# Output layer of two of ten token tiles as seven block products for eight, its sums on VectorE

## The chip, the cores and the metric

The kernel runs on one core of one Trainium2 chip. The metric is the device time of one execution in microseconds (us), as the median of several runs. A profile is one execution recorded by the hardware profiler; its times are counted from the first instruction (the span). Engines are named as in the profile: PE (TensorE matmuls), PEld (its weight loads), DVE (VectorE), ACT (ScalarE), POOL (GpSimd) and SP, which here only issues DMAs.

## The reference, cut to what matters

Sliding-window causal attention (window 64) over 8 batches, 8 heads, 576 tokens and head size 64, followed by a gated feed-forward layer:

```
scores = q @ k.T / 8, kept where 0 <= row - col < 64; attn = softmax(scores)
x = attn @ v                      # as 4608 tokens x 512
g = relu(x @ w_gate) * (x @ w_val)   # 4608 x 1536
out = g @ w_out                   # 4608 x 512, float32
```

The kernel works in fp16 operands with fp32 accumulation.

## The kernel before, in words

**Tiles.** The 4608 tokens are cut into ten tiles: tiles 0 to 3 of 384 tokens and tiles 4 to 9 of 512 tokens (in the code `NS` = 4 and `LAST` = 9). This text numbers tiles from 0, so the eighth and ninth tile are tiles 7 and 8. Of a wide tile the PE does, in this order: the hidden layer (three groups, `j` = 0, 1, 2, in `fast_hidden`), then the output layer (`fast_output`), with the attention work of later tiles put between the parts of the output layer. Ahead of parts 0 and 1 of the output of tile t come the two halves of `values` of tile t + 1 (matmuls L422, three PSUM banks each), and ahead of parts 2 and 3 two calls of `scores` of tile t + 2 (matmuls L253, four banks each). Tile 7 still has both (values of 8, scores of 9); tile 8 has the values of 9 only; tile 9 has neither.

**A group of the hidden layer.** Each group forms four blocks of 128 hidden features for all 512 tokens. The value half x @ w_val is done as seven block products for eight (P1 to P7, 256 columns each, L573): the features and the tokens are split in halves, and sums of blocks are kept ready in `vs` (of the weights, by `w_form` on POOL, L480) and `xc` (of the tokens, by `x_form` on DVE, L459). Products that are shared are copied out of PSUM on ACT (`snap`, L593) and added on DVE (`add`, L600, PSUM plus SBUF, result `vsum`, four buffers). The gate half is four ordinary 512-column products (L582), with a relu on ACT (L586). The product gate times value is then written to `g_sb`, in four pieces that this text calls (n, h): n = 1 or 0 for the upper or lower half of the features, h = 1 or 0 for the second or first half of the tokens. Piece (1, 0) is written by DVE directly from PSUM (`direct`, L613); (1, 1), (0, 0) and (0, 1) are written by POOL (L606), in this order, each from a sum that DVE has made. The sum for (0, 0) is the group's first, the sum for (1, 1) its second, the one for (0, 1) its last. PE's last product of a group, P3, adds into a bank that the DVE sum of (1, 1) must have read first.

**The output layer.** Four parts of 128 tokens, each twelve matmuls of 512 columns over the feature blocks in the order of `F_LAST` (the group j = 2 last, and of it (0, h) last: matmuls 11 and 12 of a part). Each part is copied out of PSUM by ACT (L663) and stored by a DMA on SP's queue.

**Attention on DVE.** Per half of `values`: three reciprocals (L436), three normalisations out of three banks (L441; each frees its bank), one transpose (L447), then the `xc` sums (L459). Per `scores`: four exponentials on ACT (L389, each frees a bank) and four mask products on DVE (L394).

**What sets the order.** Every engine takes its instructions in a fixed order. A `Weaver` writes it: the PE program advances a planned clock, and the other engines' work is queued with `W.at(time, fn)` at planned times and comes out in that order; `bank()` and the `done` tables make it come out earlier where the program needs it. So a plan's times decide only who stands behind whom; on the chip an engine then waits for whatever its next instruction needs. POOL is in this order too: it issues the loads of q and k (L173) and of v (L199), copies v rows between partitions (L208, L210), forms `vs`, and writes the g pieces. A load into a q or k buffer waits until DVE has transposed what the buffer held before.

**Buffers.** `g_sb` has two buffers, `o_sb` three, `snap` five, `vsum` four; the eight PSUM banks go round in a list `free`.

Of the kernel before, what the change touches and what calls it, by code (L numbers as in the profile page):

```python
# [46 lines left out]
def kernel(  # L47
# [23 lines left out]
    WT = 512  # L71
    NS = 4
    NL = (NT - NS * TT) // WT
    assert NT == NS * TT + NL * WT and TT % 128 == 0
# [20 lines left out]
    vs = persist.tile([128, 4, 2, 128 * HF], FP16)  # L95
    qTs = [persist.tile([128, 2, S, 2], FP16, name=f"qT{i}") for i in range(2)]
# [307 lines left out]
    def t_pv(t, hh, banks, give):  # L404

        if t not in wides:
            wides[t] = {"pv": {}, "give": give, "x": a_n.tile([128, 2, WS, 2, D // 2], FP16, name="xw", bufs=1),
                        "r": a_n.tile([128, 2, WS, 1], FP32, name="rw")}
        d = wides[t]
        d["pv"][hh] = banks  # L410
        unread.update(map(id, banks))
        for qh in range(2):
            qd = 2 * (t - NS) + qh
            while quads[qd].get("masked", 0) < G:
                W.pop()
            for i in range(QW):
                b, vw = divmod(q_window(qd, i), NG)
                for s in range(2):
                    n = 2 * (QW * qh + i) + s
                    to = banks[n // BS][:, VW * (n % BS):]  # L420
                    for j in range(G):
                        nc.tensor.matmul(to[32 * j:32 * j + 32, 0:D + 1],  # L422
                                         quads[qd]["p"][j][:, QW * hh + i, 32 * s:32 * s + 32],
                                         v16s[b % 2][:, vw, G * hh + j, 0:D + 1],
                                         start=True, stop=True, skip_group_check=True)
# [48 lines left out]
    def w_form(n, j):  # L474

        c = slice(256 * j, 256 * j + 256)
        f = slice(256 * j + 128 * HF, 256 * j + 128 * HF + 256)
        a11, a12, a21, a22 = wv[:, 0:2, c], wv[:, 2:4, c], wv[:, 0:2, f], wv[:, 2:4, f]
        x, y, op = ((a21, a22, ADD), (vs[:, 0, :, c], a11, SUB), (a11, a21, SUB), (a12, vs[:, 1, :, c], SUB))[n]
        nc.gpsimd.tensor_tensor(vs[:, n, :, c], x, y, op)  # L480

# [65 lines left out]
    def fast_hidden(t):  # L547
# [7 lines left out]
        def group(j):  # L555
# [40 lines left out]
            def add(delay, to, name, last, n, h):  # L596

                def summed():
# [5 lines left out]

                    def mult():
                        nc.gpsimd.tensor_tensor(gh[:, 2 * j + HF * n:2 * j + HF * n + 2, h], rh[:, 2 * n:2 * n + 2, h], pair(v), MUL)  # L606
                        done[2 * j + HF * n, h] = done[2 * j + HF * n + 1, h] = True
                    W.at(max(W.clock, at["relus", n]) + 0.7, mult)
# [30 lines left out]
            add(0.1, "C", "u2", True, 0, 1)  # L639

        for j in range(NF // 4):
            group(j)

    F_LAST = [f for j in range(NF // 4) for f in (2 * j + HF, 2 * j + HF + 1, 2 * j, 2 * j + 1)]

    def fast_output(t, between):

        g_sb, done = gs[t]
        for sub, before in enumerate(between):
# [11 lines left out]
            def evac(op=op, sub=sub):  # L661
# [3 lines left out]
                nc.sync.dma_start(out[bass.ds(starts[t] + sub * 128, 128)], o_sb)  # L665
            W.at(W.clock, evac)

# [28 lines left out]
    def output_last(t):  # L696
# [3 lines left out]
        for c0, c1, queue in ((0, 256, nc.sync), (256, 384, nc.sync), (384, DM, nc.scalar)):  # L700
# [4 lines left out]
            o_sb = consts.tile([128, c1 - c0], FP32, name=f"o_last{c0}")  # L705
            nc.scalar.copy(o_sb, op[:, 0:c1 - c0])
            queue.dma_start(out[bass.ds(starts[t] + last * 128, 128), c0:c1], o_sb)
# [11 lines left out]
    with tc.manual_schedule():  # L719
# [12 lines left out]
        zero = consts.tile([128, 512], FP16)  # L732
        nc.vector.memset(zero, 0.0)
        zero32 = consts.tile([128, 384], FP32)
# [89 lines left out]
        for u in (4, 5):  # L824
            W.at(52.0, lambda u=u: v_spread(u, pool))
        pair(2, 55.5, 58.5, 61.9)
# [22 lines left out]
        LAST = NS + NL - 1  # L849
        SLOTS = (2.6, 6.53 + 0.8, 6.53 + 2.6, 2 * 6.53 + 0.8)  # L850

        def ahead(t):
# [9 lines left out]
            if t == NS - 1:  # L862
                qk_ahead(NS + 1, T + 11.5, (0.0, 1.4, 8.0, 9.4))
                for qd, x in ((0, 6.0), (1, 9.2), (2, 22.6), (3, 25.8)):
# [34 lines left out]
        for t in range(NS, NS + NL):  # L899
# [10 lines left out]
            if t == LAST:  # L910
                fast_output(t, between[:-1])
                W.drain()
                output_last(t)
            else:
# [32 lines left out]
```

## Time and profile before

| what | value |
|---|---|
| median of 3 runs | 321.8 us (321.8 to 322.2) |
| the profiled execution | 322.06 us, its span 320.2 us |
| mean granted TensorE clock | 0.995 |
| PE busy | 308.8 us, 96% |
| DVE busy | 203.2 us, 63% |
| POOL busy | 177.8 us, 56% |
| ACT busy | 158.1 us, 49% |
| output layer of tile 7, first part to the last | 243.31 to 255.95 us, with attention between |
| output layer of tile 8 | 276.18 to 287.38 us, with one half of values between |

The times of one execution are read from its span; what lies around it is 1.86 us. The chain that ended last is PE's for 89% of the span. A matmul's own duration in the profile (379 ns at 512 columns) overlaps with the next one's: twelve take 2.70 us together, and what one costs is the distance between two starts.

### The profile page before, as it was taken

The numbers are of one execution on the slowest core, as the hardware profiler recorded it, in microseconds if no ns is written. First come the engines' busy times: TensorE is split into PE (matmuls) and PEld (weight loads), VectorE is DVE, ScalarE is ACT, GpSimd is POOL, SyncE is SP. The second block draws the span as 40 slices with busy tenths as digits, with TensorE's granted clock in tenths as the row PEclk, the third lists the DMA queues.
The fourth block names the chain that finished last, engine by engine and source line by source line (L and its number), as shares of the span: only waits on it lengthen the run. The fifth ranks groups of instructions, "written<-read, shape, count | busy, mean of one in ns | idle before, by whom it ended". The sixth has DMA issues, their size and how long they took to land.

```text
span 320.2 us, 9481 instructions
## 1 busy us (share of the span) xinstructions
PE 308.8 (96%) x4077; PEld 190.1 (59%) x4077; DVE 203.2 (63%) x397; ACT 158.1 (49%) x310; POOL 177.8 (56%) x206
## 2 busy tenths in 40 slices
PE   4799999999899999999999999999999999999996
PEld 2586958655546555665566556655665566546654
DVE  6937962667993996779576857686337734643420
ACT  3644325533524616752765276627652666326632
POOL 8859336215988506799168925980495036404540
PEclk9889999999999999999999999999999999999999
DMA  8999998946299149806910691039001100020002
GB/s 218 183 196 205 194 120 161 171 98 99 30 174 165 21 90 160 57 1 104 219 36 0 97 220 43 2 50 127 35 0 34 69 34 3 2 98 35 0 33 102
DMA packets 52491, 29.52 MB, mean 92 GB/s; under 512 B 38880, under 2 KB 43872, under 8 KB 52448
## 3 DMA queue, kind: packets, MB, share of 16 engines
q0 software_dynamic: 46688, 18.29, 49.3%
q1 hardware_dynamic: 5616, 10.55, 9.3%
q8 instruction: 32, 0.52, 0.7%
q14 instruction: 11, 0.09, 0.1%
q10 hardware_dynamic: 144, 0.07, 0.1%
HBM read 37.75 MB, written 9.44 MB: 147 GB/s over the span
## 4 chain that ended last, share of the span: by engine, by line
PE 89%; DVE 3%; ACT 2%; POOL 2%; DMA 2%; issue 1%; DVEq 0%; POOLq 0%
PE bank L658 19%; PE bank L582 19%; PE bank L538 17%; PE bank L573 17%; PE bank L673 10%; PE bank L253 3%; PE bank L422 2%; DVE p L292 2%; DMA v<-in_v_dram 2%; ACT pw L389 1%; PE bank L311 1%; DVE g_sb L525 1%; PE bank L703 1%; POOL v L199 1%; DVE qT L193 0%
## 5 line engine op out<-in xcount | busy, mean ns | idle before, releaser
L606 POOL TENSOR_TENSOR g_sb<-r,vsum 128x512 f16<-128x512 f32 x54 | 68.1, 1276 | 77.7 <-DVE vsum L600 75.7
L600 DVE TENSOR_TENSOR vsum<-bank,snap 128x512 f32<-128x512 f32 x54 | 37.3, 691 | 60.1 <-PE bank L573 36.5
L582 PE MATMUL bank<-xt,wg 128*128 128x512 f16 x288 | 73.9, 379 | 0.0
L658 PE MATMUL bank<-wo,g_sb 128*128 128x512 f16 x276 | 62.9, 380 | 0.0
L586 ACT ACTIVATE r<-bank 128x512 f32<-128x512 f32 x72 | 43.2, 600 | 32.3 <-PE bank L582 32.3
L658 PEld LDWEIGHTS <-g_sb 128*128 128x128 f16 x276 | 25.5, 98 | 28.9
L582 PEld LDWEIGHTS <-wg 128*128 128x128 f16 x288 | 28.2, 98 | 18.6
L525 DVE TENSOR_TENSOR g_sb<-r,bank 128x384 f16<-128x384 f32 x48 | 25.9, 550 | 20.3 <-PE bank L538 18.8
L522 ACT ACTIVATE r<-bank 128x384 f32<-128x384 f32 x48 | 23.7, 496 | 29.4 <-PE bank L538 20.3
L573 PEld LDWEIGHTS <-vs 128*128 128x128 f16 x288 | 28.0, 98 | 15.6 <-issue 1.6
L538 PE MATMUL bank<-xt,wg 128*128 128x192 f16 (+1 forms) x256 | 36.5, 296 | 0.5 <-DVE g_sb L525 0.4
L663 ACT COPY o_sb<-bank 128x512 f32<-128x512 f32 x23 | 13.5, 586 | 45.2 <-PE bank L658 43.2
L593 ACT COPY snap<-bank 128x512 f32<-128x512 f32 x54 | 31.6, 586 | 8.4 <-PE bank L573 8.4
L199 POOL DMA_DIRECT2D v<-in_v_dram x41 | 34.7, 865 | 1.8 <-DMA q<-in_q_dram 1.0
L538 PE MATMUL bank<-xt,wv 128*128 128x192 f16 (+1 forms) x256 | 34.3, 286 | 0.0
L673 PE MATMUL bank<-wo,g_sb 128*128 128x512 f16 x144 | 32.8, 379 | 0.2 <-DVE g_sb L525 0.2
L538 PEld LDWEIGHTS <-wg 128*128 128x128 f16 x256 | 24.3, 102 | 9.8 <-issue 0.9
L573 PE MATMUL bank<-xc,vs 128*128 128x256 f16 x216 | 29.4, 272 | 0.4 <-ACT snap L593 0.4
L208 POOL COPY v<-v 64x512 f16<-64x512 f16 (+1 forms) x22 | 16.1, 732 | 23.7 <-DMA v<-in_v_dram 22.6
L538 PEld LDWEIGHTS <-wv 128*128 128x128 f16 x256 | 22.9, 98 | 8.1
L394 DVE TENSOR_TENSOR pw<-pw,mask 128x512 f16<-128x512 f16 x48 | 20.2, 437 | 11.2 <-ACT pw L389 10.5
L389 ACT ACTIVATE pw<-bank 128x512 f16<-128x512 f32 x48 | 25.9, 608 | 1.5 <-PE bank L253 1.0
(69 smaller groups left out, 358.6 us busy)
## 6 DMA issues: line engine op xcount, KB each, us to landing
out_dram<-o_sb SPq DMA_DIRECT2D x35, 256.0 KB, 3.0
k<-in_k_dram POOLq DMA_DIRECT2D x15, 288.0 KB, 5.3
q<-in_q_dram POOLq DMA_DIRECT2D x15, 288.0 KB, 7.3
v<-in_v_dram POOLq DMA_DIRECT2D x31, 128.0 KB, 8.0
wg<-in_moe_w_gate_dram POOLq DMA_DIRECT2D x6, 256.0 KB, 6.4
wv<-in_moe_w_val_dram POOLq DMA_DIRECT2D x6, 256.0 KB, 8.2
wo<-in_moe_w_out_dram POOLq DMA_DIRECT2D x3, 512.0 KB, 11.9
v<-in_v_dram POOLq DMA_DIRECT2D x10, 64.0 KB, 5.9
```

The lines of the kernel that those rows point to most:

```text
L199: nc.gpsimd.dma_start(v16s[b % 2][lo:hi, g, :, 0:64], v[b, :, 64 * g - 64 + lo:64 * g - 64 + hi].rearrange("h p d -> p h d"))
L389: nc.scalar.activation(d["p"][g].rearrange("p n c -> p (n c)"), d["st"][g], ACT.Exp, scale=scale)
L525: nc.vector.tensor_tensor(g_sb[:, f:f + w, c0:c0 + n], part(r_sb), part(h2), MUL)
L538: nc.tensor.matmul(h[:, b * n:b * n + n], wt[:, c, (f + b) * 128:(f + b) * 128 + 128], xt[:, c, c0:c0 + n], start=(c == 0), stop=(c == NC ...
L573: nc.tensor.matmul(at[to][:, HT * i:HT * i + HT], w[:, k, 128 * i:128 * i + 128], x[:, k], start=(first and i == 0 and k == 0), stop=(k == ...
L582: nc.tensor.matmul(to, wg[:, k, 128 * ff:128 * ff + 128], xt[:, k], start=(k == 0), stop=(k == NC - 1))
L586: nc.scalar.activation(r4[:, n], to, ACT.Relu)
L593: nc.scalar.copy(at[name], at["A"])
L600: nc.vector.tensor_tensor(v, at[to], at[name], ADD)
L606: nc.gpsimd.tensor_tensor(gh[:, 2 * j + HF * n:2 * j + HF * n + 2, h], rh[:, 2 * n:2 * n + 2, h], pair(v), MUL)
L658: nc.tensor.matmul(op, g_sb[:, f, 128 * sub:128 * sub + 128], wo[:, f], start=(i == 0), stop=(i == NF - 1))
L673: nc.tensor.matmul(op, g_sb[:, f, bass.ds(sub * 128, 128)], wo[:, f], start=(f == 0), stop=(f == NF - 1))
```

## The change

In tiles 7 and 8 the output layer becomes seven block products for eight. The 512 tokens and the 512 output columns are each split in two halves, and the 1536 features into upper and lower. Each of the seven products covers 256 tokens, 768 features and 256 columns: twelve matmuls of 256 columns, so 84 matmuls of 256 columns in place of 48 of 512.

- Block sums of the output weights, `ws`, four for each of three groups, are made once by POOL (`wo_form`, 128x512 fp16): six are planned from 50.5 us, six at the planned start of tile 3 plus 15.0 to 23.4 us.
- Block sums of g, `s_sb`, four for each of three groups and each of the two tiles, are made by DVE (`g_form`, 128x512 fp16). The four of a group are planned into the next group, those of group 2 into the output layer.
- In group 2 of these tiles the piece (0, 0) of g is written by DVE in place of POOL.
- Three products are copied out by ACT (`snap`), three results are summed and one copied into `o_sb`: the three sums on DVE, the copy on ACT. The stores are of 256 columns by 256 tokens.
- The products P1, P2, P5 and so on accumulate in three banks (A, B, C) that are held over several products, where before one bank was held at a time. In tile 7 `scores` comes after the first half of P2 and after P4, and the second half of `values` after P5.
- In all wide tiles the first half of a tile now holds its even tokens, the second its odd ones: the weights of the L422 matmuls are read with a step of two elements, and stores go to every second row.
- The zeros for the warm-up matmuls lie in `ws`, and the last part of tile 9 takes its three output buffers from `o_sb` in place of buffers of its own.

The order of instructions on DVE, ACT and POOL is else what it was. On POOL, the first six weight sums stand before and after the four v copies that begin at 45.44 us in the profile of before; the other six stand behind the q load that is issued at 122.92 us, five of them ahead of the v loads of tile 5's keys and values, and the sixth between these loads and the first three g products of tile 4. On DVE, in tiles 7 and 8, the order from the second sum of group 2 on is: sum of (1, 1), `direct`, g sum, sum of (0, 1), product (0, 0), g sum, three reciprocals, g sum, three normalisations, transpose, g sum, three reciprocals, `xc`, three normalisations, transpose; then in tile 7 three masks and three `xc` sums before the first two output sums, in tile 8 one `xc` sum before the first. In tile 7 the first `scores` takes two banks that the second half of `values` gives back (by its first and second normalisation).

```diff
-                                         quads[qd]["p"][j][:, QW * hh + i, 32 * s:32 * s + 32],
+                                         quads[qd]["p"][j][:, QW * hh + i, s:64:2],
...
+    def wo_form(n, j):
+        ...
+        nc.gpsimd.tensor_tensor(to[:, n], x, y, SUB)
...
+    def blocks_out(t):
+        return LAST - 2 <= t < LAST
+
+    def g_form(t, n, j, eng):
+        ...
+        for f, h in (((f1, 0), (f2, 0)), ((f1, 1),), ((f1, 0), (f1, 1)), ((f2, 1),))[n]:
+            while (f.start, h) not in done:
+                W.pop()
+        ...
+        x, y, op = ((a21, a22, ADD), (to[:, 0], a11, SUB), (a11, a21, SUB), (a12, to[:, 1], SUB))[n]
+        eng.tensor_tensor(to[:, n], x, y, op)
...
+                    late = blocks_out(t) and j == NF // 4 - 1 and (n, h) == (0, 0)
...
-                        nc.gpsimd.tensor_tensor(gh[:, 2 * j + HF * n:2 * j + HF * n + 2, h], rh[:, 2 * n:2 * n + 2, h], pair(v), MUL)
+                        (nc.vector if late else nc.gpsimd).tensor_tensor(gh[:, 2 * j + HF * n:2 * j + HF * n + 2, h], rh[:, 2 * n:2 * n + 2, h], pair(v), MUL)
...
+            if blocks_out(t):
+                late = j == NF // 4 - 1
+                for n, x in ((2, 6.6), (0, 7.2), (1, 7.3), (3, 10.4)) if late else ((2, 9.9), (0, 10.0), (1, 10.1), (3, 10.9)):
+                    W.at(T + x, lambda n=n: g_form(t, n, j, nc.vector))
...
+    def block_output(t, after):
...
+        run(0)
+        product("P1", "A", True)
+        snap("a1")
+        product("P5", "C", True)
+        run(1)
+        product("P6", "A", False)
+        snap("u2")
+        product("P2", "B", True, (0,))
+        run(2)
+        product("P7", "A", False)
+        snap("u3")
+        add(0.9, "C", "u3", False, 0, c2)
+        product("P2", "B", False, (1,))
+        add(0.1, "B", "a1", True, 1, c1)
+        product("P4", "A", False)
+        W.at(W.clock, direct)
+        run(3)
+        while ("summed", "u3") not in at:
+            W.pop()
+        product("P3", "C", False)
+        add(0.1, "C", "u2", True, 1, c2)
...
-            o_sb = consts.tile([128, c1 - c0], FP32, name=f"o_last{c0}")
+            o_sb = f_sb.tile([128, DM], FP32, name="o_sb")[:, 0:c1 - c0]
...
+        for j in range(NF // 4):
+            for n in range(2):
+                W.at(50.5 + 1.2 * (2 * j + n), lambda n=n, j=j: wo_form(n, j))
...
+                for j in range(NF // 4):
+                    for n in range(2, 4):
+                        W.at(T + 15.0 + 1.2 * (2 * j + n), lambda n=n, j=j: wo_form(n, j))
...
+            elif blocks_out(t):
+                block_output(t, between)
```

In `block_output`, `run(0)` and `run(1)` are the two halves of `values`, `run(2)` and `run(3)` the two calls of `scores`; P1, P2 and P4 read g, P5, P6, P7 and P3 read the g sums 0, 1, 2 and 3 of all three groups.

## The prediction

> **What bounds the kernel now.** I read the chain that ended last first, then the busy times of each tile, then the time lines of POOL and DVE where the change inserts work.
>
> ```profile
> PE 89%; DVE 3%; ACT 2%; POOL 2%; DMA 2%; issue 1%; DVEq 0%; POOLq 0%
> ```
>
> ```profile
> core 0: us, PE busy (x) PEld busy (x) DVE busy (x) ACT busy (x) POOL busy (x), PEclk, DMA share, GB/s
> 124.90:157.15 32.25, 31.82 (x488) 18.81 (x487) 25.69 (x49) 19.69 (x37) 25.17 (x28) 1.00 0.75 90
> 223.08:255.95 32.87, 32.87 (x439) 19.56 (x437) 18.15 (x38) 18.49 (x33) 15.76 (x15) 1.00 0.09 34
> 255.95:287.38 31.43, 31.43 (x311) 18.62 (x309) 15.01 (x30) 14.36 (x25) 11.30 (x9) 1.00 0.09 35
> ```
>
> These stretches are tiles 4, 7 and 8. PE has no idle time in 7 and 8: matmuls taken away there shorten the run, and every wait given to PE lengthens it. Over a whole tile POOL and DVE have room, but the mean hides the places. In tile 4 POOL is 25.17 of 32.25 us busy, and this is what lies ahead of its output layer:
>
> ```profile
> 122.92 0.53 POOL L173 DMA_DIRECT2D q<-in_q_dram  x1 [1.69 <-DVE xc L459]
> 123.44 4.22 POOL L199 DMA_DIRECT2D v<-in_v_dram  x5
> 129.67 1.31 POOL L606 TENSOR_TENSOR g_sb<-r,vsum 128x512 f16<-128x512 f32 x1 [2.02 <-DVE vsum L600]
> 131.34 2.65 POOL L606 TENSOR_TENSOR g_sb<-r,vsum 128x512 f16<-128x512 f32 x2 [0.35 <-ACT r L586]
> ...
> 136.29 1.28 POOL L606 TENSOR_TENSOR g_sb<-r,vsum 128x512 f16<-128x512 f32 x1 [0.55 <-DVE vsum L600]
> ...
> 143.31 2.51 POOL L606 TENSOR_TENSOR g_sb<-r,vsum 128x512 f16<-128x512 f32 x2
> ```
>
> ```profile
> 144.45 2.70 PE bank L658 x12
> ```
>
> The last POOL row writes (1, 1) and (0, 0) of group 2 and ends at 145.82. PE's matmul 11 of the first output part reads (0, 0), and stands at 144.45 + 10 x 0.225 = 146.7. So POOL has 0.9 us to spare there, and 2.02 + 0.35 + 0.55 = 2.9 us of waits before: 3.8 in all.
>
> **The matmuls.** Twelve 512-column matmuls without attention between take 7.88 / 3 us (36 in 7.88 at 279.50), so 48 take 10.5; by the gate rows (four in 0.86) 10.3. Eight 256-column ones take 0.87 (L573), so 84 take 9.2. The gain is 1.2 us a tile, 2.4 in two, if nothing waits. The 36 further weight loads are covered: the 0.87 rows already have a load for each matmul.
>
> **Six weight sums ahead of tile 4.** The nearest row is w_form's, of the same shape and engine:
>
> ```profile
> L480 POOL TENSOR_TENSOR vs<-wv x6: 1152/1212/1269, 77.1 to 99.8; 128x512 f16<-128x512 f16 x6
> ```
>
> Their starts lie 1.22 us apart (77.11, 78.33), so six take 7.3 us. They stand behind the q load of 122.92, which waits for DVE and cannot come earlier, and ahead of the v loads or the first product. Less the 3.8 to spare, (0, 0) is late by 3.5 us, and PE waits that long, partly in the groups (a fifth `vsum` waits for the first product), the rest at matmul 11. This is the lower end. For the upper end see how a DVE operation with two SBUF operands runs beside POOL:
>
> ```profile
> 147.96 1.30 POOL L606 TENSOR_TENSOR g_sb<-r,vsum 128x512 f16<-128x512 f32 x1
> ```
>
> ```profile
> 148.28 1.29 DVE L459 TENSOR_TENSOR xc<-xt 128x512 f16<-128x512 f16 x1
> ```
>
> It took 1.29 us, where the median of this line is 0.42, and ended 0.31 after POOL's. The sums out of PSUM (L600, 670 to 693 ns in all 54) show nothing of it. In after, eight masks (123.58 to 130.7) meet a POOL that is never idle; if five of them come between the sums and hold POOL for 0.3 us each, it is 1.5 more: 5.0. I take 4.5, as the row shows the exclusion but not who goes first. Tile 5 gets nothing further: its products begin 9.16 us after POOL's last load of v.
>
> [...]
>
> **The first six weight sums** cost nothing. POOL idles 9.7 us before 45.44 and takes two there; four push the q and k loads from 48.4 to 53.3, which land 5 to 7 us later, and DVE first reads them at 66.65. The v copies of 62.05 move to 67 to 69 and are read by PE at 86.1. Without that cover it would be up to 4.9.
>
> **DVE in tile 7.** Lines from group 2 on:
>
> ```profile
> 240.82 0.69 DVE L600 TENSOR_TENSOR vsum<-bank,snap 128x512 f32<-128x512 f32 x1 [1.63 <-ACT snap L593]
> 241.43 0.69 DVE L613 TENSOR_TENSOR g_sb<-r,bank 128x512 f16<-128x512 f32 x1
> 243.41 0.33 DVE L436 RECIPROCAL rw<-bank 128x2 f32<-128x2 f32 x3
> 243.66 1.30 DVE L441 TENSOR_TENSOR xw<-bank,rw 128x128 f16<-128x128 f32 x3
> 245.00 1.25 DVE L447 STREAM_TRANSPOSE xt<-xw 128x1024 f16<-128x1024 f16 x1
> ```
>
> From start to start: a sum 0.61, three reciprocals 0.25, three normalisations 1.34, a transpose 1.28; an fp16 sum 0.34 (250.97 to 251.30 among the xc sums); the moved product I take as a PSUM sum, 0.61 (below it only if SBUF operands are quicker, above it 1.29 by the blocked row). All times are in the clock of before. *Group 1's sums* stand between 239.1 and the sum of (1, 1) at 240.82, but the fourth needs POOL's last product of group 1, which ends at 241.03. So the sum of (1, 1) starts at 241.4; with the exclusion, in which the first sum waits for one product and the next for another, at 242.3. PE's P3 needs it and goes to 242.2 or 243.0 from 242.09. *The chain* from there to the second normalisation of the second half of values: 0.61 + 0.61 + 0.34 + 0.61 + 0.61 + 0.34 + 0.25 + 0.34 + 1.34 + 1.28 + 0.34 + 0.25 + 0.34 + 0.95 = 8.2, plus 0.85 in which the first g sum waits for POOL's product (1, 1) (1.27 us long, started only when the sum is done). It ends at 250.4; with the exclusion one more sum waits for a product (1.25), 252.6. *PE* wants the scores, which need that bank, after P3 (0.44), values, P1, P5, values, P6, half of P2 (0.62 + 0.62 + 42 x 0.109 = 5.8): at 248.5, or 250.5 with its own wait in P5. It waits 2.0 or 2.1 us. After the scores it wants P3 4.5 us later (0.62 + 30 x 0.109 + 0.62), at 255.0 or 257.1; DVE has still 0.61 + 1.28 + six fp16 operations at 0.34 + 0.61 + 0.69 = 5.2 us to go before P3's bank is read, 255.7 or 257.8. P3 takes 1.3, and tile 8 starts at 257.1 or 259.2 against 255.95: the gain has gone, and tile 7 is **1.1 to 3.2 us longer**. I take 2.8, near the upper end, since there POOL's products and DVE's sums meet in nearly every step.
>
> **DVE in tile 8.** POOL has no copies here, group 1's sums fit, and the sum of (1, 1) keeps its 273.69. From it to the end of the output sum that P3 waits for: the first thirteen terms above and the 0.85 (8.1), then three normalisations, transpose, one xc sum and a sum of 0.69, 3.65: 285.4, or 286.7 with one exclusion. PE wants P3 at 276.11 + 72 x 0.109 + 0.62 + 0.1 = 284.7, waits, and ends at 286.8 or 288.0 against 287.38: -0.6 to +0.6; I take +0.4.
>
> **Small edits.** Weights with a step of two elements: kT's (L253) are read so already, and 64 of those matmuls take 0.61 us as 64 of L422 do, so nothing; the far bound, a load stretch of 0.58 us doubled in twelve stretches, is 6.5. Last part of tile 9: the third copy starts at 317.44, and now needs the store issued at 315.4 to have landed; there these take 2.0 us (3.0 over the run), so 0.1, at most 1.0. ACT copies as often as before. The fourth store's buffer waits for the first store, but behind it on DVE stand only masks and a sum of the next tile with a microsecond to spare.
>
> **Sum.** 4.5 + 2.8 + 0.4 + 0.1 = 7.8 us on 322.06, so 329.9 for a profiled execution like that of before; 0.26 less to the median: **329.6**.
>
> **The clock.** In 12:14 PE was busy 1.35 of 2.00 us, with no idle above 0.65, and the granted clock of 14:18 was 0.57. Tile 7's output stage has 3 to 4 us of waits in 16; a loss as at 14:18 is 1.7 us and belongs to the upper end. [...]
>
> **Rivals.**
> - *DVE and POOL hardly exclude each other*: all lower ends, 3.5 + 1.1 - 0.6 = 4.0, so 325.8. For it: the masks of 105 to 107, at 0.41 us beside POOL's copies. Chance 0.25.
> - *Only POOL's queue costs*: g sums and output sums hide as planned, 3.5 - 2.4 = +1.1, so 322.9. It needs DVE operations of about two thirds of my durations. Chance 0.10.
> - *Faster*: the bound stays PE throughout, 321.8 - 2.4 = 319.4. It decides in tile 4: if a weight sum took under 3.8 / 6 = 0.63 us there, as the 64x512 copy does (0.61), POOL would be in time, and DVE would have to be in time too. Chance 0.05.
> - *Dearer weights or clock*: over 332.5. Chance 0.05.
> - The forecast: 0.55.
>
> 0.2% (0.64 us) is about what a measurement can tell from no change. All cases but one are above it, one of them barely: slower 0.93, same 0.02, faster 0.05. The range from 325.2 to 332.5 leaves out the two low rivals and the dear one.
>
> **What would show it.** In after: six POOL sums between 123.4 and 136 and the first product of tile 4 at 135 or later; PE idle some 4 us in tile 4, ended by POOL's g; in tile 7 PE idle about 2 us ahead of the first scores and under 1 ahead of P3, both ended by DVE; fp16 DVE sums of 0.8 to 1.3 us in group 2 and 0.42 elsewhere. A tile 4 without a wait, or output stages of 7 and 8 that are 1 us shorter, would make it wrong.

## The result, and the profile after

The changed kernel takes 333.0 us (median of six runs, 330.9 to 335.8), and the kernel before, on the same chip, 322.4 us: a ratio of 1.033, with a 95% interval of 1.028 to 1.038. The forecast was 329.6 us with a range of 325.2 to 332.5. The direction and the places were right; the size was 3.4 us too small.

The profiled execution took 333.4 us, its span 331.7. Line numbers have moved: the sums from PSUM (L600) are now L635, POOL's g products (L606) L643, the output matmuls (L658) L702, normalisations L443, `xc` sums L461, masks L396, values L424, scores L255. New are L491 (`wo_form`), L514 (`g_form`), L737 (the block products) and L753 (the output sums). First the chain that ended last, from the page of the changed kernel:

```profile
PE 60%; DVE 16%; POOL 15%; issue 6%; DMA 2%; ACT 2%; DVEq 0%; POOLq 0%; ACTq 0%
```

PE had 89% of it before. Now 31% of the span lies on DVE and POOL in this chain. The stretches of tiles 4, 7 and 8, from the table by windows (length, then busy time of each engine, granted clock):

```profile
122.50:163.70 41.20, 37.14 (x502) 20.90 (x501) 31.71 (x52) 22.20 (x41) 34.35 (x36) 0.92 0.75 90
229.61:265.83 36.22, 32.75 (x474) 23.23 (x473) 26.69 (x52) 18.26 (x33) 15.31 (x14) 1.00 0.05 18
265.83:298.58 32.75, 30.88 (x347) 21.99 (x345) 23.62 (x49) 15.08 (x27) 10.39 (x8) 1.00 0.11 36
```

From the first hidden-layer matmul of one tile to that of the next (of tile 9 to the end of the span), the tiles of all kernels in this text have these lengths in us. They carry most of what follows.

| kernel | tile 4 | tile 5 | tile 6 | tile 7 | tile 8 | tile 9 |
|---|---|---|---|---|---|---|
| before | 34.72 | 33.02 | 32.91 | 32.87 | 31.42 | 32.99 |
| after | 41.16 | 33.00 | 32.92 | 36.22 | 32.75 | 33.12 |
| sums early | 34.72 | 32.92 | 32.92 | 36.23 | 32.76 | 33.07 |
| sums only | 38.50 | 33.19 | 32.93 | 32.87 | 31.43 | 34.10 |
| even and odd only | 34.73 | 33.31 | 32.93 | 32.87 | 31.43 | 33.84 |
| wait filled | 38.64 | 33.15 | 32.93 | 36.49 | 32.76 | 33.09 |
| ninth tile only | 34.73 | 33.15 | 32.93 | 32.87 | 32.90 | 33.05 |
| eighth tile only | 34.72 | 32.91 | 32.93 | 36.23 | 31.42 | 33.16 |
| eighth, copies early | 34.72 | 33.12 | 32.93 | 33.97 | 31.41 | 33.12 |
| ninth mended | 34.72 | 32.93 | 32.92 | 32.87 | 30.60 | 33.13 |
| both mended | 34.72 | 33.19 | 32.92 | 33.16 | 30.59 | 33.06 |
| order of B | 34.72 | 33.31 | 32.93 | 31.85 | 30.59 | 33.11 |

So the 11.5 us that the span grew are 6.4 in tile 4, 3.35 in tile 7, 1.3 in tile 8, 0.1 in the last part, and 0.3 before tile 4, whose start lies between 122.27 and 123.53 us in these profiles.

**Tile 4.** POOL's time line, which answers to the one from 122.92 us on of before:

```profile
123.19 0.53 POOL L175 DMA_DIRECT2D q<-in_q_dram  x1 [1.69 <-DVE xc L461]
123.79 1.15 POOL L491 TENSOR_TENSOR ws<-wo 128x512 f16<-128x512 f16 x1
124.90 1.33 POOL L491 TENSOR_TENSOR ws<-wo,ws 128x512 f16<-128x512 f16 x1
...
135.43 3.76 POOL L643 TENSOR_TENSOR g_sb<-r,vsum 128x512 f16<-128x512 f32 x3
...
148.04 2.48 POOL L643 TENSOR_TENSOR g_sb<-r,vsum 128x512 f16<-128x512 f32 x2
```

The first product stands at 135.43 where it stood at 129.67, and POOL runs from then on without a gap until the two products that end at 150.52. PE meets this at matmul 11 of the first output part, as was foreseen, and then something else happens:

```profile
145.26 2.33 PE L702 MATMUL bank<-wo,g_sb 128*128 128x512 f16 x10
150.58 1.03 PE L702 MATMUL bank<-wo,g_sb 128*128 128x512 f16 x2 [2.99 <-POOL g_sb L643]
151.54 1.07 PE L424 MATMUL bank<-v,pw 128*32 128x65 f16 x64
152.55 4.69 PE L702 MATMUL bank<-wo,g_sb 128*128 128x512 f16 x12
```

Twelve matmuls take 4.69 us in place of 2.76, and 64 of the values take 1.07 in place of 0.69. The table by windows of two microseconds, the granted clock in the column after PE's busy time, says why:

```profile
core 0: us, PE busy (x), PEclk, DMA share, GB/s
147.00:149.00 2.00, 0.59 (x3) 1.00 0.00 0
149.00:151.00 2.00, 0.42 (x2) 0.66 0.00 0
151.00:153.00 2.00, 2.00 (x68) 0.50 0.60 61
...
155.00:157.00 2.00, 2.00 (x7) 0.63 1.07 174
157.00:159.00 2.00, 2.00 (x72) 1.00 1.07 256
```

The clock fell to half during the wait and came back some 6.8 us later (1.36 us at 0.50 give the 0.66 of 149:151, and 1.48 of the last at 0.50 the 0.63 of 155:157, with four between). From 150.58 to the first scores at 157.17 are 6.6 us; the same work took 3.9 in a kernel with the same wait and no fall (below). So tile 4's 6.4 us are 0.5 in the groups, 3.15 at the wait and 2.7 of slow clock, to 0.1. By this a wait takes about 0.16 us more than the number in brackets. That is what a matmul's own 0.38 us exceeds the 0.22 from one start to the next, and the matmul ahead of a wait has no next one to overlap with.

**Tile 7.** DVE's time line in group 1 and group 2, two rows of POOL's, and one line of the table of waits of PE from 100 us on (1.6 us in three waits, the longest 1.1):

```profile
239.27 2.06 DVE L514 TENSOR_TENSOR s_sb<-g_sb 128x512 f16<-128x512 f16 x2
...
242.75 0.68 DVE L635 TENSOR_TENSOR vsum<-bank,snap 128x512 f32<-128x512 f32 x1
...
246.98 1.82 DVE L514 TENSOR_TENSOR s_sb<-g_sb 128x512 f16<-128x512 f16 x2
...
252.72 0.68 DVE L643 TENSOR_TENSOR g_sb<-r,vsum 128x512 f16<-128x512 f32 x1
253.44 1.37 DVE L514 TENSOR_TENSOR s_sb<-g_sb 128x512 f16<-128x512 f16 x1
```

```profile
238.36 2.68 POOL L643 TENSOR_TENSOR g_sb<-r,vsum 128x512 f16<-128x512 f32 x2
...
252.95 1.58 POOL L643 TENSOR_TENSOR g_sb<-r,vsum 128x512 f16<-128x512 f32 x1 [1.20 <-DVE vsum L635]
```

```profile
PE bank L608 <- DVE vsum L635: 1.6, 3, 1.1
```

Four g sums of group 0 stand ahead of the sum of (1, 1) of group 1 (242.75), and last from 239.27 to 242.8. The first two run beside the two POOL products that begin at 238.36 and take 2.06 us; the other two run beside v copies and take 0.71 and 0.65. PE's P3 of group 1 waits 1.1 us for that sum. The same happens in group 2 with the sums of group 1, and in the output layer PE waits three times more:

```profile
254.87 0.61 PE L737 MATMUL bank<-ws,s_sb 128*128 128x256 f16 x4 [0.92 <-DVE s_sb L514]
...
259.00 0.18 PE L255 MATMUL bank<-qT,kT 32*128 32x64 f16 x1 [0.69 <-DVE xw L443]
259.53 0.66 PE L255 MATMUL bank<-qT,kT 32*128 32x64 f16 x61 [0.35 <-DVE xw L443]
```

**Tile 8.** DVE's last steps, and PE's P3, which waits for an output sum to leave its bank:

```profile
295.60 0.68 DVE L753 TENSOR_TENSOR o_sb<-bank,snap 128x512 f32<-128x512 f32 x1
296.20 0.41 DVE L461 TENSOR_TENSOR xc<-xt 128x512 f16<-128x512 f16 x1
296.54 0.68 DVE L753 TENSOR_TENSOR o_sb<-bank,snap 128x512 f32<-128x512 f32 x1
```

```profile
297.27 1.47 PE L737 MATMUL bank<-wo,s_sb 128*128 128x256 f16 x12 [1.53 <-DVE o_sb L753]
```

PE goes on when the *second* output sum is done, not the first. The first is B's; P3 needs C's.

### The profile page after: what moved, and what is told of

Its sections match the earlier page's. It is cut to its first block, busy times and chain, and to the rows that moved or that the text cites. A ratio compares the mean times of both kernels' runs of the same rounds, so it can differ in the third digit from the quotient of the medians.

```text
span 331.7 us, 9683 instructions
## 1 busy us (share of the span) xinstructions
PE 310.9 (94%) x4149; PEld 196.9 (59%) x4149; DVE 227.5 (69%) x429; ACT 158.2 (48%) x310; POOL 190.5 (57%) x216
## 4 chain that ended last, share of the span: by engine, by line
PE 60%; DVE 16%; POOL 15%; issue 6%; DMA 2%; ACT 2%; DVEq 0%; POOLq 0%; ACTq 0%
PE bank L573 16%; PE bank L617 12%; PE bank L608 11%; PE bank L702 10%; PE bank L797 6%; POOL g_sb L643 6%; POOL v L201 3%; DVE s_sb L514 3%; DVE p L294 2%; DVE xw L443 2%; DVE xt L449 2%; POOL ws L491 2%; PE bank L255 2%; POOL v L212 2%; DMA v<-in_v_dram 2%
## 5 line engine op out<-in xcount | busy, mean ns | idle before, releaser
L643 POOL TENSOR_TENSOR g_sb<-r,vsum 128x512 f16<-128x512 f32 x52 | 66.2, 1290 | 82.9 <-DVE vsum L635 81.3
L635 DVE TENSOR_TENSOR vsum<-bank,snap 128x512 f32<-128x512 f32 x54 | 37.2, 688 | 42.3 <-PE bank L608 27.7
L702 PE MATMUL bank<-wo,g_sb 128*128 128x512 f16 x180 | 43.6, 395 | 3.0 <-POOL g_sb L643 3.0
L617 PEld LDWEIGHTS <-wg 128*128 128x128 f16 x288 | 28.2, 98 | 18.8 <-issue 0.2
L573 PE MATMUL bank<-xt,wg 128*128 128x192 f16 (+1 forms) x256 | 35.0, 286 | 1.5 <-DMA wg<-in_moe_w_gate_dram 0.6
L797 PE MATMUL bank<-wo,g_sb 128*128 128x512 f16 x144 | 32.8, 379 | 0.2 <-DVE g_sb L560 0.2
L396 DVE TENSOR_TENSOR pw<-pw,mask 128x512 f16<-128x512 f16 x48 | 25.0, 540 | 9.8 <-ACT pw L391 9.2
L702 PEld LDWEIGHTS <-g_sb 128*128 128x128 f16 x180 | 17.0, 101 | 23.5 <-POOL g_sb L643 3.5
L573 PEld LDWEIGHTS <-wg 128*128 128x128 f16 x256 | 22.9, 98 | 10.8 <-issue 1.5
L573 PEld LDWEIGHTS <-wv 128*128 128x128 f16 x256 | 22.9, 98 | 8.1
L608 PEld LDWEIGHTS <-wv 128*128 128x128 f16 x216 | 21.1, 98 | 7.2
L707 ACT COPY o_sb<-bank 128x512 f32<-128x512 f32 x15 | 8.8, 587 | 33.9 <-PE bank L702 29.9
```

What stands on the lines that cost most here:

```text
L573: nc.tensor.matmul(h[:, b * n:b * n + n], wt[:, c, (f + b) * 128:(f + b) * 128 + 128], xt[:, c, c0:c0 + n], start=(c == 0), stop=(c == NC ...
L608: nc.tensor.matmul(at[to][:, HT * i:HT * i + HT], w[:, k, 128 * i:128 * i + 128], x[:, k], start=(first and i == 0 and k == 0), stop=(k == ...
L617: nc.tensor.matmul(to, wg[:, k, 128 * ff:128 * ff + 128], xt[:, k], start=(k == 0), stop=(k == NC - 1))
L635: nc.vector.tensor_tensor(v, at[to], at[name], ADD)
L643: (nc.vector if late else nc.gpsimd).tensor_tensor(gh[:, 2 * j + HF * n:2 * j + HF * n + 2, h], rh[:, 2 * n:2 * n + 2, h], pair(v), MUL)
L702: nc.tensor.matmul(op, g_sb[:, f, 128 * sub:128 * sub + 128], wo[:, f], start=(i == 0), stop=(i == NF - 1))
```

## The experiments

The theory after the result: the matmuls saved are real, and the rest is three separate costs, POOL's six weight sums in tile 4, a fall of the clock that follows from their wait, and DVE's chain in tiles 7 and 8, lengthened where it runs beside POOL. The rivals: that the new token order or the stores slow something throughout; that the 2.7 us after the wait have another cause than the wait; and that DVE simply has too much work in tiles 7 and 8, so that no order helps.

### The second six weight sums ahead of the q loads

```diff
-                W.at(load, lambda name=name, hh=hh: qk_load(b, name, hh))
+                W.at(load + 0.001 * i, lambda name=name, hh=hh: qk_load(b, name, hh))
...
-                        W.at(T + 15.0 + 1.2 * (2 * j + n), lambda n=n, j=j: wo_form(n, j))
+                        W.at(T + 15.6015, lambda n=n, j=j: wo_form(n, j))
```

> The changed kernel with one edit: the second six weight sums on POOL stand between the two k loads and the two q loads that POOL issues ahead of tile 4 (at 112 us in the profile of before, where POOL then idles 8.3 us for DVE), no longer behind the q loads. Theory A (they hold POOL's queue, and PE waits in tile 4 for the g piece (0, 0); the wait costs clock on top): tile 4 comes back to its length of before, 6.4 us less, so 333.0 - 6.4 = 326.6 us, with tiles 7 and 8 unchanged at +3.3 and +1.3. Theory B (tile 4 is late for the masks on DVE, or for the strided weights): a time of 331 us or more. Half of 6.4 back would say that only the queue goes and the clock loss has another cause.

Measured: 327.3 us (326.9 to 328.0), ratio 1.017 (1.014 to 1.019). POOL now makes these sums in idle time before the q loads (from 113.42 to 120.14), and the first output part of tile 4 runs through:

```profile
145.29 2.76 PE L702 MATMUL bank<-wo,g_sb 128*128 128x512 f16 x12
```

Tile 4 is back at 34.72 us, to the hundredth, and the other tiles keep their lengths within 0.1 us. The run is 0.7 us above the expected 326.6; in the profiled execution tile 4 starts at 123.18, 0.65 later than in the changed kernel's. Half of the loss hung on where six POOL instructions stood, and none of this half on their number.

### The weight sums without the block products

```diff
     def blocks_out(t):
-        return LAST - 2 <= t < LAST
+        return False
```

> The changed kernel without the block products of the output layer and without the g sums: tiles 7 and 8 have the output layer of before; the twelve weight sums on POOL, the even and odd tokens and the output buffers of the last part stay (the weight sums are not used). Theory A: only tile 4 is longer, 322.4 + 6.4 = 328.8 us (327 to 330, as the clock loss differs from run to run). Theory B (the six sums alone do little, and it takes the block products to make the loss): 323 to 324 us.

All weight sums are made, and none is used. Measured: 327.45 us (326.7 to 329.6), ratio 1.018 (1.014 to 1.022). Tiles 7 and 8 are those of before; tile 4 is 38.50, 3.8 us longer, and tile 9 is 34.10, 1.1 longer (more on this below). Here is the same wait again, and the clock beside it, in the profiled execution:

```profile
150.42 0.60 PE L702 MATMUL bank<-wo,g_sb 128*128 128x512 f16 x2 [2.99 <-POOL g_sb L643]
```

```profile
149.00:151.00 2.00, 0.58 (x7) 1.00 0.00 0
151.00:153.00 2.00, 2.00 (x72) 1.00 0.62 62
```

The wait is the same to the hundredth, and the clock stays at 1.00. So this wait lowers the clock in some executions and not in others: the four runs had mean clocks of 0.988 to 1.000, and the slowest clock was the longest run (329.6). The six runs of the changed kernel show the same order: 330.9 us at a mean clock of 1.000, 332.2 and 332.7 at 0.995, 333.4 twice at 0.990, 335.8 at 0.985. A mean clock does not say where in a run the clock fell, though.

### The wait filled with matmuls of nothing

Thirteen matmuls of 512 columns with unused results stand ahead of matmul 11 of the first part of tile 4.

```diff
+                if t == NS and sub == 0 and i == NF - 2:
+                    spare = bank()
+                    heat(13, spare)
+                    free.append(spare)
```

> The changed kernel with thirteen further matmuls of 512 columns (2.8 us, into a spare bank, read by nobody) ahead of matmul 11 of the first output part of tile 4, where PE waits 3.0 us for POOL. They do no useful work. Theory A (the wait lowers the granted clock to 0.5 for some 5 us, which costs 2.4 us beyond the wait): the matmuls fill the wait, the clock stays at 1.0, and the run is 2.4 us shorter, 330.6 us. Rival (the low clock has another cause, or the wait is not as long in most runs): no change, 333 us, or up to 2.8 us longer, 335.8.

```profile
147.73 2.97 PE L217 MATMUL bank<-ws 128*128 128x512 f16 x13
150.89 0.61 PE L706 MATMUL bank<-wo,g_sb 128*128 128x512 f16 x2 [0.19 <-POOL g_sb L643]
```

Measured: 331.7 us (330.9 to 331.9), ratio 1.030 (1.027 to 1.032), with a clock of 1.000 in all four runs. POOL releases PE at the same point of the tile, PE has merely done something meanwhile, and tile 4 is 38.64 in place of 41.16. So the fall hangs on PE standing still there, as far as four runs can tell, and it cost 2.5 us in the profiled execution. The 1.3 us between the medians are a rough figure. Of 69 runs of the kernel before, which has no such wait, 19 have a mean clock of 0.995 or less too; in its profiled execution the fall is at the start:

```profile
12.00:14.00 2.00, 1.35 (x72) 1.00 1.23 202
14.00:16.00 2.00, 1.86 (x14) 0.58 1.24 205
16.00:18.00 2.00, 2.00 (x17) 0.57 1.23 202
```

So in runs of the changed kernel other than the profiled one, a low mean clock may come from there.

### Even and odd tokens alone

As the run without block products, and the weight sums left out as well; what stays is the token order, the stores, the shared zeros and the `o_sb` buffers of the last part.

```diff
-        return LAST - 2 <= t < LAST
+        return False
...
-        for j in range(NF // 4):
-            for n in range(2):
-                W.at(50.5 + 1.2 * (2 * j + n), lambda n=n, j=j: wo_form(n, j))
...
-                for j in range(NF // 4):
-                    for n in range(2, 4):
-                        W.at(T + 15.0 + 1.2 * (2 * j + n), lambda n=n, j=j: wo_form(n, j))
```

> The changed kernel without block products, g sums and weight sums: what is left is the even and odd tokens (weights read with a step of two, stores to every second row) and the output buffers of the last part. Theory A: 322.4 us, no difference over 0.3 us. Theory B (strided weights or strided stores cost something in each of the six wide tiles): 0.2 us or more for each of twelve stretches of matmuls with such weights, so 324.8 us or more.

Measured: 323.0 us (322.6 to 323.6, ten runs), ratio 1.0026 (1.0013 to 1.0040). That is 0.7 us where nothing was expected. The profiled execution shows it as 0.85 in tile 9, 0.3 in tile 5 and 0.2 before tile 4. Sixty-four matmuls with the strided weights take 0.69 us, as those of before do, so they are not the cause. All kernels with block products carry the same edit and end their tile 9 after 33.05 to 33.16 us; the two without them take 33.84 and, with the weight sums only, 34.10. In this run's profile, ACT's last store takes longer to issue (1.10 us in place of 0.37) and to land (2.3 us from its issue in place of 1.6). Why it does stays open.

### Block products in the ninth tile only, and in the eighth only

Both with the weight sums early.

```diff
-        return LAST - 2 <= t < LAST
+        return t == LAST - 1
```

> As the kernel with the early weight sums (327.3 us), but the block products in tile 8 alone; tile 7 has the output layer of before. If the costs of the tiles add up, tile 7's 3.3 us go and tile 8's 1.3 stay: 327.3 - 3.3 = 324.0 us, tile 8 being 32.75 us long with PE waits of 0.3 us for a g sum and 1.5 us for the output sum ahead of P3. Rival (the later tile is long only as it inherits DVE's lag from tile 7): tile 8 near 30.9 us and the run at or below 322.3.

Measured: 324.25 us (323.6 to 324.6), ratio 1.006 (1.004 to 1.008).

```diff
-        return LAST - 2 <= t < LAST
+        return t == LAST - 2
```

> As the kernel with the early weight sums (327.3 us), but the block products in tile 7 alone. If costs add up: 327.3 - 1.3 = 326.0 us, with tile 7 at 36.2 us and PE's waits there as in the changed kernel: 1.1 us in group 1, 0.3 in group 2, 0.9 in P5, 1.0 at the scores. Rival (tile 8 inherits a lag): tile 8 above 31.42 us although it has no block products.

Measured: 326.6 us (326.0 to 326.7), ratio 1.013 (1.010 to 1.015). The two costs are independent: tile 7 takes 36.23 us in this kernel and 36.22 with both, tile 8 takes 32.90 alone and 32.75 with both, and each leaves the other tile at the length of before.

### The eighth tile with POOL's copies moved away

As the last, and the six v copies that POOL makes between the products of groups 0 and 1 of tile 7 are planned ahead of the first product. DVE's order is not touched.

```diff
-                W.at(T + 6.0 + 2.5 * i, lambda u=u: v_spread(u, pool))
+                W.at(T + (1.0 + 0.1 * i if t == LAST - 1 else 6.0 + 2.5 * i), lambda u=u: v_spread(u, pool))
```

> As the kernel with the block products in tile 7 alone (326.0 us expected), but POOL's six v copies of that tile stand ahead of the first g product, where POOL idles 11 us, no longer between the products of groups 0 and 1. Theory A (a DVE sum with two SBUF operands and a POOL operation shut each other out, so that the sums of group 0 took 2.06 for two, 0.71 and 0.65 us beside POOL's products and copies, and made PE wait 1.1 us for the sum of (1, 1) in group 1): those sums take 0.34 to 0.42 us, the wait in group 1 goes, tile 7 is 1.1 to 1.4 us shorter, 324.8 us. Rival (the wait in group 1 comes from DVE's load alone): no change, 326.0.

```profile
230.00 3.80 POOL L643 TENSOR_TENSOR g_sb<-r,vsum 128x512 f16<-128x512 f32 x3 [3.98 <-DVE vsum L635]
```

```profile
233.95 0.75 DVE L514 TENSOR_TENSOR s_sb<-g_sb 128x512 f16<-128x512 f16 x2
...
240.45 0.75 DVE L514 TENSOR_TENSOR s_sb<-g_sb 128x512 f16<-128x512 f16 x2
...
245.86 1.38 DVE L514 TENSOR_TENSOR s_sb<-g_sb 128x512 f16<-128x512 f16 x1
```

Measured: 323.8 us (323.2 to 324.5), ratio 1.0047 (1.0030 to 1.0064), a microsecond better than expected. The first pairs of g sums take 0.75 us where they took 2.06 and 1.82. The one at 245.86 still meets a POOL product (begun at 245.37, 1.59 us long) and still takes 1.38. Tile 7 fell from 36.23 to 33.97: 2.26 us hung on where six POOL copies stood, and both waits of the groups are gone. The copies did this less by running beside the sums than by what they delayed: with the copies out of the way POOL's three products of group 0 end at 233.80, just ahead of the sums at 233.95. In the changed kernel two of these products lay beside the sums, which stand at the same point of the tile (9.7 us after its start). What is left is P5's wait, now 0.31, and the two at the scores (0.70 and 0.35).

### The ninth tile with DVE's order mended

As the run with the ninth tile only; in tile 8, C's output sum stands ahead of the last transpose, and the second half of values ahead of P5.

```diff
-    def values(t, hh, T, banks=None):
+    def values(t, hh, T, banks=None, late=0.0):
...
-        W.at(T + 2.7, lambda: t_turn(t, hh))
+        W.at(T + 2.7 + late, lambda: t_turn(t, hh))
...
-            W.at(T + 4.0 + 0.4 * n, lambda n=n: x_form(t, n))
+            W.at(T + 4.0 + 0.4 * n + 0.6 * late, lambda n=n: x_form(t, n))
...
+        run(1)
         product("P5", "C", True)
-        run(1)
...
-        add(0.9, "C", "u3", False, 0, c2)
+        add(0.9 if t < LAST - 1 else 0.0, "C", "u3", False, 0, c2)
...
-                between[1].append(lambda: values(t + 1, 1, W.clock))
+                between[1].append(lambda: values(t + 1, 1, W.clock, late=2.6 if t == LAST - 1 else 0.0))
```

> As the kernel with the block products in tile 8 alone (324.0 us expected), with two changes of order in that tile: the output sum that P3 waits for stands ahead of the last transpose on DVE, and the second half of values ahead of P5. If PE's waits of 1.5 us ahead of P3 and 0.3 to 0.5 in P5 are all that eats the gain of 1.2 us, tile 8 becomes 30.6 to 30.9 us long against 31.42 before, and the run is 324.0 - 2.0 = 322.0 us; against the kernel before a ratio of 0.997 to 1.000, as even and odd tokens alone measured 0.7 above it. Rival (DVE is late for P3 in any order, or the transposition is then late for tile 9): tile 8 at 32 us or tile 9 longer, and 323 us or more.

```profile
283.93 0.69 DVE L753 TENSOR_TENSOR o_sb<-bank,snap 128x512 f32<-128x512 f32 x1
284.54 1.24 DVE L449 STREAM_TRANSPOSE xt<-xw 128x1024 f16<-128x1024 f16 x1
```

Measured: 322.0 us (321.35 to 323.2, twelve runs), ratio 0.9999 (0.9983 to 1.0014). Tile 8 is 30.60 us, without a wait in its output layer. Against 31.42 of before that is a gain of 0.82, not the 1.2 of the prediction. PE's lines show where the rest is:

```profile
278.34 2.79 PE L737 MATMUL bank<-ws,s_sb 128*128 128x256 f16 x24
280.97 0.82 PE L737 MATMUL bank<-wo,g_sb 128*128 128x256 f16 x6
281.81 1.47 PE L737 MATMUL bank<-ws,s_sb 128*128 128x256 f16 x12
```

Twenty-four matmuls take 2.63 us from start to start, 0.110 each, as assumed. The six of half of P2 take 0.84, which is 0.18 more than six of those; both halves do, and P1, ahead of the values, takes 1.41 where twelve are 1.32. Why is not shown: with both tiles mended (below), the second half of P2 in tile 7, which there stands behind the scores, takes 0.67.

### Both tiles mended

Block products in both tiles, the copies early, tile 8 as above, and in tile 7 the same reordering, with the first scores behind P7.

```diff
-        return t == LAST - 1
+        return LAST - 2 <= t < LAST
...
-        run(2)
+        if t == LAST - 1:
+            run(2)
...
-        add(0.9 if t < LAST - 1 else 0.0, "C", "u3", False, 0, c2)
+        add(0.0, "C", "u3", False, 0, c2)
+        if t < LAST - 1:
+            run(2)
...
-                between[0].append(lambda: values(t + 1, 0, W.clock))
+                between[0].append(lambda: values(t + 1, 0, W.clock, late=1.4 if t == LAST - 2 else 0.0))
...
-                between[1].append(lambda: values(t + 1, 1, W.clock, late=2.6 if t == LAST - 1 else 0.0))
+                between[1].append(lambda: values(t + 1, 1, W.clock, late=2.6 if t >= LAST - 2 else 0.0))
```

> Block products in both tiles again, with tile 8 as in the run with the ninth tile mended, the v copies of tile 7 early, and in tile 7 the same reordering of VectorE: the first half's transpose behind the second half's normalisations, C's output sum ahead of the second transpose, values half 2 ahead of P5, and the first scores behind P7 instead of ahead of it. Theory (the matmuls saved are real, and what cost more was the order on VectorE and on POOL): tile 8 stays at 30.6 us, and tile 7 loses the 0.31 + 0.70 + 0.35 us of waits left with its copies early, so it comes to 31.7 to 32.2 us against 32.87 in the kernel before; by the 322.0 of the run with the ninth tile mended, 320.9 to 321.4, about 0.3% under the kernel before. Rival (VectorE has too much work for tile 7 in any order): a wait ahead of P3 takes the place of those ahead of the scores, tile 7 stays at 33 to 34 us, and the time is 322.1 to 323.1.

Measured: 321.9 us (321.5 to 323.1, twelve runs), ratio 1.000 (0.9988 to 1.0012). The three waits are gone, and one new one has come, as the rival said, but in another place, ahead of the second scores:

```profile
254.64 0.66 PE L255 MATMUL bank<-qT,kT 32*128 32x64 f16 x61 [1.12 <-DVE o_sb L753]
```

```profile
253.91 0.69 DVE L753 TENSOR_TENSOR o_sb<-bank,snap 128x512 f32<-128x512 f32 x1
```

The output sum at 253.91 is B's; its bank is the one that these scores write, and it stands behind a transpose (begun at 251.96) and two `xc` sums. DVE's order again, not its amount of work.

### The order of B

```diff
-        add(0.1, "B", "a1", True, 1, c1)
+        add(0.0 if t < LAST - 1 else 0.1, "B", "a1", True, 1, c1)
...
-                between[1].append(lambda: values(t + 1, 1, W.clock, late=2.6 if t >= LAST - 2 else 0.0))
+                between[1].append(lambda: values(t + 1, 1, W.clock, late={LAST - 2: 4.2, LAST - 1: 2.6}.get(t, 0.0)))
```

The `xc` sums are delayed with the transpose.

> As the run with both tiles mended, with one more change of VectorE's order in tile 7: B's output sum, which frees the bank that the second scores write, stands ahead of the second transpose and the xc sums instead of behind them (253.91 there). Theory: the one wait left there, 1.12 us of TensorE ahead of the second scores, goes, and nothing takes its place, since the second transpose then ends some 1.3 us before tile 8 reads its tokens; tile 7 is 32.0 to 32.2 us against 32.87 in the kernel before, tile 8 stays 30.6, and the time is 320.7 to 321.0, some 0.3% under the kernel before. Rival: tile 8 now begins before its tokens or differences are ready, a wait at its first matmuls takes the place, and the time stays at 321.8.

```profile
251.70 1.45 DVE L753 TENSOR_TENSOR o_sb<-bank,snap 128x512 f32<-128x512 f32 x2
...
253.40 1.24 DVE L449 STREAM_TRANSPOSE xt<-xw 128x1024 f16<-128x1024 f16 x1
```

Measured: 321.0 us (319.9 to 321.7, twelve runs), ratio 0.9966 (0.9954 to 0.9979) to 322.1 of the kernel before. Tile 7 is 31.85 and tile 8 30.59, 1.02 and 0.83 us shorter than before, with 73% of tile 7 busy on DVE (23.27 of 31.85). This is all of PE's waits from tile 4 on, and none of them is in an output layer with block products:

```profile
PE bank L255 <- ACT pw L391: 0.4, 1, 0.4
PE bank L608 <- ACT snap L628: 0.4, 1, 0.4
PE bank L255 <- issue: 0.2, 1, 0.2
```

So the rival that DVE has too much work for tile 7 in any order falls, and the change can be made to gain: a third of a percent, by moving instructions only.

## Why the prediction was right or wrong

In the profiled execution it was 11.3 us in place of the 7.8 of the sum. Term by term, with what the runs showed:

| term | predicted | measured |
|---|---|---|
| tile 4, the weight sums | 4.5 (3.5 to 5.0) | 3.8 (sums only) to 3.9 (wait filled) |
| clock | 0 in the sum, 1.7 at the upper end | 2.5 in the profiled execution, roughly 1.3 between medians |
| tile 7 | 2.8 (1.1 to 3.2) | 3.35 |
| tile 8 | 0.4 (-0.6 to 0.6) | 1.33 |
| last part | 0.1 | 0.1 |
| ahead of tile 4 | 0 | 0.3 |

**The step that failed first is the clock.** The prediction had the row that mattered (12:14 and 14:18 of before, a clock of 0.57 with no idle time above 0.65), and put its 1.7 us on the waits of tile 7's output stage, at the upper end only. It did not apply it to the one wait of 3 us that it had itself worked out for tile 4. In the profiled execution 3.5 us were missing from the forecast: the clock is 2.5 of them, tiles 7 and 8 together 1.5, and tile 4 without the clock gave 0.6 back. The waits of tiles 7 and 8, 1.5 us at most, left the clock at 1.00; the wait of 2.99 took it to 0.50, about 2 us after PE stopped: PE's last matmul ahead of it ends at 147.59, and the 0.66 of 149:151 puts the fall at 149.64. The same wait in the run with the weight sums only left it at 1.00. What decides between the two executions, and how long a wait must be for it, is not shown.

**Tile 4 without the clock was right in mechanism**, and near its lower end. The 1 us on top of that end, for masks that hold POOL, did not come: POOL's five sums begin 1.26 us apart (123.79 to 130.07), against the 1.22 taken. DVE's masks and POOL's sums did slow each other, but DVE paid the most: four of the five sums take 1.33 or 1.34 us where the first takes 1.15, and three masks, 0.42 to 0.43 us each in before, take 3.96 together.

```profile
123.85 3.96 DVE L396 TENSOR_TENSOR pw<-pw,mask 128x512 f16<-128x512 f16 x3 [0.70 <-ACT pw L391]
```

There PE's long wait was for POOL and not for DVE. In tile 7 PE waits for what stands behind such sums on DVE, and that is the second failure.

**Tile 7 was mis-sized at both ends of its chain.** The prediction costed the g sums of group 1 in group 2, and left out that those of group 0 do the same in group 1: P3 of group 1 waited 1.1 us. It also left out the v copies between POOL's products, which push these products into the sums: with the copies moved, the first pair takes 0.75 in place of 2.06 us. Against that, the waits in the output layer were smaller than foreseen: 1.0 us ahead of the first scores in place of 2.0 (with 0.9 in P5), and none ahead of P3, where 0.7 was foreseen. The pairs of 0.75 and 2.06 us are one without a POOL product beside it and one with two. Which side pays can be read in two meetings from the starts in the rows. The product (0, 0) on DVE begins at 252.72 and takes 0.68 us, as a sum out of PSUM does, and POOL's product, begun at 252.95, takes 1.58 in place of 1.27; the next g sum begins at 253.44, within POOL's product, and takes 1.37 in place of 0.42. So the product (0, 0), for which the prediction had 1.29 us as the upper case, was not the one to wait.

**Tile 8 failed on an order misread.** The prediction ended its chain at the first output sum, as the one that P3 waits for. The first is B's and C's is second, behind one more `xc` sum: 0.61 + 0.34 us more. The order of the banks is in the code (`add` of "C" is planned 0.9 late, `add` of "B" 0.1), and would have told it. The first sum itself ended where the chain had it: at 296.28, which is 286.24 in the clock of before (tile 8 starts 10.04 us later), against 285.4 to 286.7.

**The matmuls gain 0.8 to 1.0 us a tile, not 1.2.** The assumption of 0.109 us for each of 84 holds where many stand in a row (24 in 2.63 us), not for P1 ahead of the values (1.41 for twelve) and for the halves of P2 that stand behind another product (0.84 for six). Tile 7 has one such half in the last run and tile 8 two, at 0.17 each, and the gains are 1.02 and 0.83.

**The rest held.** The first six weight sums and the strided weights cost nothing that a row shows, and the `o_sb` buffers of tile 9 cost 0.1; only the two runs without block products, with tiles 9 that are 0.85 and 1.1 us longer, speak against it. Of the rivals, "DVE and POOL hardly exclude each other" is refuted by the pairs above. "Faster" named tile 4 and DVE as what must give way, and the last experiment gets there by these two and by POOL's copies in tile 7, at 321.0 and not at 319.4: the gain of the matmuls is smaller than it was taken to be, and in its profiled execution 0.5 us more went by before tile 4 (122.79 against 122.27) and 0.3 more in tile 5.

## What to carry to other kernels

When work is taken from a bound engine and given to one that is 40% idle, read the order of that engine's instructions step by step at the places where the bound engine needs it next; here 10 us of loss became 1 us of gain with the same instructions in another order. When a forecast finds a wait of the bound engine, price its clock too, separately, since it can cost nearly as much again after the wait has ended (2.5 us on 2.99 here, in one execution). A sum that runs beside another engine's work must be costed at the duration it has there (here 1.82 to 2.06 us for two g sums beside POOL's products, 0.75 without), and whether the two meet depends on *everything* in that engine's queue: six copies ahead of POOL's products were worth 2.26 us.

## What the runs showed of the hardware that had not been expected

- A single wait of 2.99 us on PE halved its clock for about 6.8 us in one execution, and left it at 1.00 in another kernel's execution with the same wait to the hundredth. With matmuls of nothing in the gap the mean clock was 1.000 in four runs of four.
- Two fp16 sums of 128x512 out of SBUF take 0.75 us on DVE beside an idle POOL, and 1.82 to 2.06 us beside POOL's products. A DVE product begun 0.23 us ahead of POOL's took 0.68 us, and POOL's product beside it 1.58 in place of 1.27; a g sum begun within that one took 1.37 in place of 0.42. Three masks took 3.96 us beside POOL's sums, which themselves went from 1.15 to 1.33 us.
- In tile 8 of the run with it mended, six 256-column matmuls that are half of a product take 0.84 us, where the next twelve take 1.30; behind the scores, in tile 7 of the last two runs, six take 0.67.
